# Attention and a max-of-three FFN on one core: another written order of commands, other engines for copies and masks, other places for the K and Q loads

## The chip, the cores and the metric

The kernel runs on one core of a Trainium2 chip. The metric is the device time of one execution in microseconds (us), the median of several runs. A core has five engines that run side by side, each through its own stream of instructions in order, and they wait for one another through semaphores: TensorE (PE in the profile; its weight loads are PEld), VectorE (DVE), ScalarE (ACT), GpSimd (POOL) and SyncE (SP), which here only issues DMAs. DMAs are issued from the queues of SP, POOL and ACT.

## The reference

Two stages. The first is attention of 4 batches with 8 heads over 768 positions and a head size of 64. Heads 0, 2 and 6 ("retrieval") see all earlier positions, the other five only the first 4 positions and the last 64. The second stage takes the 3072 rows of 512 that come out, multiplies them by three matrices, takes the largest of the three products element by element, and multiplies by a fourth matrix.

```python
scores = scale * np.matmul(q, k.transpose(0, 1, 3, 2))
stream_keep = causal & (is_sink | in_win)
scores = np.where(mask[None, :, :, :], scores, -1000000000.0)
a = np.exp(scores - max) / sum
out = np.matmul(a, v)                       # (4, 8, 768, 64)
x = out.transpose(0, 2, 1, 3).reshape(3072, 512)
h = np.maximum(np.maximum(x @ w1, x @ w2), x @ w3)   # (3072, 768)
return h @ w_out                            # (3072, 512)
```

## The kernel before

The work is cut into eight blocks (b,half): batch 0 to 3, first or second half of its 768 positions. Each block has an attention part and an FFN part, and while PE works on the FFN of one block, the attention of the next is woven in between. Nothing is planned at run time: the order is written out by hand in a list of strings, `PROGRAM` (L132). The function `run` (L895) reads it from left to right and emits each command's instructions; each engine gets its own in that order. There is a second list, `GENERAL`, for other patterns of heads; it is in the program behind a branch and isn't run here.

The commands that matter, with the functions behind them. A step t counts batch, half and a bit qd that picks four of the eight heads; i picks two heads of those.

- `ld h hp` loads K and Q of two pairs of heads of batch 0's second half in fp32 (tile kf, `load_pairs`, L293), `load b c` those of four heads of a later batch, cast to fp16 on the way (tile kq, L354). Both go through POOL's queue, in POOL's program order. `w n` loads a weight matrix there too (L556, L563). `load_v b half` loads V in three DMAs from SP, `load_vp` from POOL (tile vs, L412).
- `cast h hp e` casts K and Q of a pair in batch 0 to fp16 (L314), the two letters naming the engines (d DVE, a ACT, p POOL). `turnp h hp e` turns them on PE (L333) and copies them to KQ (L341), with one or two copies. For later batches `turn b qd i part` does the turning with a DVE transposition (L388).
- `s t u` makes scores on PE (tile st, L737) and takes exp on ACT (L748). It uses the two PSUM buffers of the pool sps, or, with a b at its end, buffers of the pool of four banks. `k t i u e` multiplies by the masks on DVE or POOL (L762 for the heads with a window, L782 and L797 for the others). `o` copies the sink columns.
- `v t i e` casts V to fp16 (va, L656) and fills the masked copy vf (L660, L665, L672); the first letter is the engine of the cast, the second that of the copies.
- `av t i` multiplies by V on PE (oacc, L823); DVE then takes the reciprocal of the sums (L831) and writes x (L834).
- `x t i e` transposes x into xT, by PE and a copy (L853, L854), or with D by a DMA from SP (L847). The FFN of a block is put into the queue when its last x is emitted.
- `f 1 e` is one step of the FFN that is first in the queue: four matmuls of 128 by 384 (yy, L591) and then either a copy on engine e (products with the first matrix, L608) or a max on DVE (L611). After 18 such steps come three outputs of six matmuls (L627), each with a copy on engine e (L633) and a DMA from SP (L634), and an empty step behind each. Block (0,·) takes all first products first, the others go round matrix by matrix.
- `gate` and `pad` put a tiny DMA into SP's queue (L398); `gate` waits for a tile of masked scores. `um` makes a mask (L533).

Ahead of the list, K and Q of batch 0's first half are issued from SP and ACT, and constants are made.

What sets who waits for whom: the order on each engine, two score buffers, four PSUM banks for everything else (yy, oacc, transpositions), three buffers of vs and of KQ, four of kf and kq together, two of x and three of xT.

```python
PROGRAM = (
    "um 1 1, cast 0 1 dp, cast 0 3 pd, turnp 0 1 a, cast 0 0 aa, s 0 0 1, ld 1 0, cast 0 2 dd",
    ...
```

Of the kernel before, what the change touches and what calls it, by code (L numbers as in the profile page):

```python
# [129 lines left out]
)  # L130

PROGRAM = (  # L132
    "um 1 1, cast 0 1 dp, cast 0 3 pd, turnp 0 1 a, cast 0 0 aa, s 0 0 1, ld 1 0, cast 0 2 dd",
    "um 0 1, s 0 1 1 b, um 1 0, turnp 0 0 aa, load_v 0 0, turnp 0 3 d, s 0 0 0, turnp 0 2 aa",
    "s 1 0 1, o 0 1 0 d, v 0 0 dd, w 0, v 1 1 dd, ld 1 2, cast 1 0 pp, s 1 1 1, cast 1 1 pp",
    "v 1 0 ad, turnp 1 0 a, w 1, s 0 1 0 b, s 1 0 0, o 0 0 0 p, av 0 0, s 1 1 0 b, av 1 1",
    "av 1 0, v 0 1 pp, um 0 0, turnp 1 1 aa, av 0 1, s 2 0 0, x 0 0 d, s 2 0 1, x 1 0 d",
    "x 0 1 a, load_vp 0 1, x 1 1 d, cast 1 3 aa, cast 1 2 dp, w 2, f 1 a, s 2 1, f 1 a",
    "turnp 1 3 d, load 1 0, f 1 d, f 1 a, s 2 2, f 1 d, turnp 1 2 da, f 1 a, k 2 0 2 d",
    "k 2 0 1 d, k 2 1 1 p, f 1 d, w 3, load 1 1, f 1 a, s 3 0, o 0 0 1 p, o 0 1 1 d, k 3 0 0 d",  # L140
    "f 1 a, v 2 1 dd, v 2 0 ad, v 3 1 ad, f 1 d, v 3 0 dp, s 3 1 0, f 1 d, f 1 d, s 2 3, f 1 a",
    "f 1 d, turn 1 0 0 1, k 3 0 1 p, k 2 0 3 p, f 1 a, f 1 a, k 2 1 3 p, av 2 0, av 3 0, f 1 a",
    "f 1 a, k 3 1 0 p, s 3 1 1, x 3 0 a, x 2 0 a, k 3 1 1 p, turn 1 0 1 0, av 2 1, gate, av 3 1",
    "load 2 0, turn 1 0 0 0, load_v 1 0, f 1 a, x 2 1 a, f 1 a, f 1 a, x 3 1 a, f 1 a, f 1 a",
    "f 1 a, f 1 a, turn 1 1 0 1, turn 1 1 0 0, load 2 1, f 1 a, turn 1 0 1 1, f 1 a",
    "turn 1 1 1 0, turn 1 1 1 1, f 1 d, f 1 a, s 4 0, f 1 d, f 1 a, f 1 d, k 4 0 0 p, s 5 0",
    "f 1 d, k 5 0 0 d, turn 2 0 0 0, k 5 1 0 p, f 1 a, f 1 d, s 5 1, o 1 1 0 p, f 1 a, f 1 a",
    "turn 2 0 1 1, load_v 1 1, s 4 1, f 1 a, o 1 0 0 p, k 4 0 1 d, turn 2 0 1 0, v 5 0 pp",
    "f 1 d, s 5 2, k 4 1 1 p, f 1 a, load_v 3 1, v 5 1 pp, v 4 0 ap, f 1 d, f 1 a, s 6 0",
    "av 4 0, k 4 1 0 d, k 5 1 2 d, v 4 1 dp, f 1 a, k 5 0 2 p, s 6 1, v 7 0 ap, av 5 0",  # L150
    "k 5 0 1 d, av 4 1, x 5 0 D, av 5 1, s 6 2, f 1 a, x 4 1 D, x 4 0 d, f 1 a, turn 2 0 0 1",
    "av 7 0, x 5 1 a, s 6 3, turn 2 1 1 0, k 6 1 1 p, v 6 1 ad, f 1 a, turn 2 1 0 0",
    "turn 2 1 0 1, load 3 1, k 6 0 3 p, f 1 a, f 1 d, k 6 1 3 p, turn 2 1 1 1, f 1 a, k 5 1 1 p",
    "k 6 0 1 p, f 1 d, f 1 a, load_v 2 0, f 1 d, av 6 1, s 8 0, f 1 d, v 7 1 pd, f 1 a, f 1 a",
    "v 6 0 dp, f 1 d, pad, s 9 0, f 1 d, f 1 a, k 8 1 0 d, turn 3 1 1 1, f 1 a, load_v 2 1",
    "f 1 d, k 9 1 0 p, s 8 1, k 6 0 2 p, turn 3 1 1 0, f 1 a, av 7 1, v 8 1 ad, f 1 a, f 1 a",
    "f 1 a, k 9 0 0 d, s 9 1, f 1 d, x 6 1 D, v 9 0 pp, v 9 1 ap, f 1 a, v 10 1 pp, av 6 0",
    "x 6 0 D, turn 3 1 0 0, o 2 1 0 p, s 10 0, x 7 0 D, k 8 0 0 d, o 2 0 0 d, v 11 1 ap, f 1 d",
    "f 1 d, v 14 0 pp, f 1 d, x 7 1 a, f 1 d, turn 3 1 0 1, v 8 0 pd, f 1 d, s 9 2, k 9 1 1 d",
    "pad, v 11 0 dp, k 8 0 1 d, f 1 a, f 1 a, k 9 0 2 d, k 9 1 2 p, f 1 d, f 1 d, f 1 a, f 1 d",  # L160
    "k 8 1 1 d, load_v 3 0, load 3 0, s 10 1, k 10 0 1 p, av 9 0, f 1 a, f 1 a, f 1 d, av 8 1",
    "k 10 1 1 d, s 10 2, v 12 1 pd, av 9 1, x 8 1 D, av 8 0, f 1 a, f 1 d, v 13 0 ap, x 8 0 D",
    "v 10 0 dd, f 1 d, f 1 d, f 1 a, s 10 3, k 9 0 1 d, f 1 d, turn 3 0 0 1, x 9 0 D, f 1 d",
    "x 9 1 D, f 1 a, f 1 a, k 10 0 2 p, f 1 a, turn 3 0 0 0, pad, f 1 d, f 1 d, f 1 a, f 1 a",
    "v 15 0 dp, f 1 a, f 1 d, turn 3 0 1 0, f 1 a, turn 3 0 1 1, f 1 d, av 11 0, v 12 0 ad",
    "k 10 1 3 d, s 12 0, f 1 d, k 10 0 3 p, f 1 a, k 12 0 0 d, f 1 d, f 1 a, s 13 0, v 14 1 pp",
    "av 10 0, f 1 d, f 1 a, s 13 1, av 10 1, k 12 1 0 p, f 1 d, k 13 1 1 p, s 14 0, f 1 d",
    "f 1 d, f 1 d, o 3 0 0 p, f 1 a, f 1 d, v 13 1 ad, s 12 1, k 12 1 1 p, x 11 0 D, x 10 0 D",
    "av 11 1, f 1 a, x 10 1 D, f 1 d, k 12 0 1 d, s 14 1, k 13 0 1 d, f 1 d, f 1 a, k 14 0 1 p",
    "x 11 1 D, f 1 a, o 3 1 0 d, k 13 0 0 d, k 13 1 0 d, f 1 a, f 1 a, av 12 0, f 1 d, s 13 2",  # L170
    "f 1 a, f 1 a, k 13 0 2 p, f 1 a, f 1 a, f 1 d, f 1 a, s 14 2, k 13 1 2 p, av 13 0, f 1 d",
    "x 13 0 D, f 1 a, f 1 d, f 1 d, av 13 1, s 14 3, x 12 0 D, av 12 1, av 15 0, f 1 d",
    "k 14 0 3 d, f 1 a, f 1 a, k 14 1 3 p, f 1 a, f 1 d, f 1 a, k 14 1 1 p, f 1 a, f 1 a",
    "x 12 1 D, v 15 1 pd, k 14 0 2 p, x 13 1 D, f 1 d, f 1 d, f 1 a, av 14 0, x 14 0 D, f 1 d",
    "x 15 0 D, av 14 1, f 1 a, av 15 1, f 1 a, f 1 d, f 1 a, f 1 d, f 1 d, f 1 a, f 1 a, f 1 a",
    "f 1 d, f 1 d, x 14 1 D, f 1 d, f 1 a, f 1 a, f 1 d, f 1 d, f 1 d, f 1 a, f 1 a, f 1 a",
    "x 15 1 D, f 1 d, f 1 d, f 1 a, f 1 a, f 1 d, f 1 d, f 1 a, f 1 a, f 1 d, f 1 a, f 1 d",
    "f 1 d, f 1 d, f 1 d, f 1 d, f 1 d, f 1 d, f 1 a, f 1 d, f 1 a, f 1 d, f 1 a, f 1 a, f 1 d",
    "f 1 d, f 1 a, f 1 a, f 1 a, f 1 a, f 1 d, f 1 a, f 1 a",
)  # L180


# [774 lines left out]
```

## Time and profile before

| what | value |
|---|---|
| median of 6 runs | 195.19 us (192.88 to 196.26) |
| profiled execution | 195.55 us, span of its instructions 193.7 us |
| mean granted clock of PE | 0.992 |
| PE busy | 178.7 us, 92% of the span |
| DVE, ACT, POOL busy | 140.2, 100.7, 80.3 us (72%, 52%, 41%) |
| DMA queues, share of 16 engines | SP 31.4%, POOL 27.4%, ACT 1.7% |
| last instruction of PE ends | 188.07 us |

The profile is of one execution. Its span goes from the first instruction to the last one or the last DMA's end, and 1.85 us of the execution lie outside it. "Busy" is the union of an engine's instructions, "idle before" is the time an engine stood before an instruction, put down to what released it. The chain that ended last is followed back from the end: at each step to what released it. A row in the timeline has start, length, engine, line, operation, result and sources.

### The profile page before, as it was taken

To read this page: it belongs to the slowest core of one execution; us is meant where nothing else is said; L and a number is where in the kernel's file an instruction comes from. 1 tells how busy PE (TensorE), PEld (TensorE's weight loads), DVE (VectorE), ACT (ScalarE), POOL (GpSimd) and SP (SyncE) were. 2 spreads that over 40 slices of the span, in tenths; PEclk is the share of its full clock that TensorE was granted. 3 is DMA by queue.
4 is the path that set the end of the run, shared out by engine and by line. 5 is a ranking of instruction groups with operands and counts; after the bars stand their busy time and mean duration, and the time that the engine had idled before them with its cause. 6 is when DMAs were issued, how large, how long until landed. Compare 5 with 4: busy or idle time off the path is not lost.

```text
span 193.7 us, 4787 instructions
## 1 busy us (share of the span) xinstructions
PE 178.7 (92%) x1887; PEld 104.7 (54%) x1887; DVE 140.2 (72%) x302; ACT 100.7 (52%) x158; POOL 80.3 (41%) x117
## 2 busy tenths in 40 slices
PE   7398799899999888999999999999999999999980
PEld 2265465665555545556565556655565656555540
DVE  4337657999689997699989987677399666638720
ACT  3289898326677991768665448656751111020030
POOL 3289572883268497086495042412807000000000
PEclk9999999999999999999999999999999999999996
DMA  5999999999998359971599940203322151030022
GB/s 157 283 230 239 231 239 213 209 219 214 182 291 186 106 72 258 183 131 33 183 187 166 67 164 3 41 4 95 112 44 42 58 169 24 0 141 22 0 110 65
DMA packets 41277, 26.02 MB, mean 134 GB/s; under 512 B 31586, under 2 KB 36258, under 8 KB 41250
## 3 DMA queue, kind: packets, MB, share of 16 engines
q1 hardware_dynamic: 34994, 14.39, 31.4%
q0 software_dynamic: 4880, 10.23, 27.4%
q10 hardware_dynamic: 1376, 1.05, 1.7%
q8 instruction: 16, 0.26, 0.6%
q14 instruction: 11, 0.09, 0.2%
HBM read 25.17 MB, written 6.29 MB: 162 GB/s over the span
## 4 chain that ended last, share of the span: by engine, by line
PE 71%; DMA 14%; DVE 5%; POOL 4%; issue 2%; ACT 2%; DVEq 0%; SPq 0%; POOLq 0%; ACTq 0%
PE yy L591 40%; PE yy L627 13%; PE st L737 6%; PE oacc L823 6%; DMA kf<-in_q_dram 5%; PE yst L591 3%; DMA ks<-in_k_dram 3%; DMA xT<-x 2%; DMA vs<-in_v_dram 2%; DMA qs<-in_q_dram 1%; POOL kf L293 1%; POOL pn L762 1%; PE yst L627 1%; ACT pn L748 1%; DVE pn L762 1%
## 5 line engine op out<-in xcount | busy, mean ns | idle before, releaser
L591 PE MATMUL yy<-xT,w0t 128*128 128x384 f16 x180 | 36.2, 326 | 2.7 <-DMA xT<-x 1.7
L591 PE MATMUL yy<-xT,w1t 128*128 128x384 f16 x180 | 35.7, 326 | 0.0
L591 PE MATMUL yy<-xT,w2t 128*128 128x384 f16 x180 | 35.5, 326 | 0.0
L748 ACT ACTIVATE pb<-st 128x1024 f16<-128x1024 f32 (+1 forms) x32 | 29.4, 972 | 7.9 <-PE st L737 7.4
L611 DVE TENSOR_TENSOR acc<-yy,acc 128x384 f16<-128x384 f32 x45 | 24.8, 557 | 11.2 <-PE yy L591 6.7
L627 PE MATMUL yy<-woutt,hT 128*128 128x512 f16 (+1 forms) x138 | 31.9, 374 | 0.0
L608 ACT CAST acc<-yy 128x384 f16<-128x384 f32 x29 | 14.0, 483 | 29.1 <-PE yy L591 29.0
L748 ACT ACTIVATE pn<-st 128x1024 f16<-128x1024 f32 (+4 forms) x27 | 22.1, 873 | 11.8 <-PE st L737 11.8
L762 POOL TENSOR_TENSOR pn<-pn,mk 128x512 f16<-128x512 f16 (+3 forms) x14 | 20.8, 1500 | 17.1 <-ACT pn L748 16.9
L611 DVE TENSOR_TENSOR hT<-yy,acc 128x384 f16<-128x384 f32 x45 | 24.6, 556 | 3.3 <-PE yy L591 0.7
L591 PEld LDWEIGHTS <-w0t 128*128 128x128 f16 x192 | 18.1, 98 | 15.7 <-issue 3.8
L388 DVE STREAM_TRANSPOSE KQ<-kq 128x384 f32<-128x384 f32 x24 | 25.4, 1134 | 0.0
L591 PEld LDWEIGHTS <-w1t 128*128 128x128 f16 x192 | 18.0, 98 | 12.2 <-issue 0.3
L591 PEld LDWEIGHTS <-w2t 128*128 128x128 f16 x192 | 18.0, 98 | 11.7 <-issue 0.4
L737 PE MATMUL st<-KQ 32*128 32x128 f16 (+5 forms) x560 | 23.4, 253 | 0.5 <-ACT KQ L341 0.5
L627 PEld LDWEIGHTS <-hT 128*128 128x128 f16 x150 | 14.0, 98 | 14.2 <-issue 0.3
L633 ACT COPY ot<-yy 128x512 f32<-128x512 f32 x16 | 9.4, 590 | 18.3 <-PE yy L627 18.3
L834 DVE TENSOR_TENSOR x<-oacc,rc 128x384 f16<-128x384 f32 x32 | 17.8, 558 | 1.5 <-DVE rc L831 0.4
L737 PEld LDWEIGHTS <-KQ 32*128 32x128 f16 (+1 forms) x560 | 11.6, 93 | 13.1 <-issue 8.8
L748 ACT ACTIVATE pa<-st 128x1024 f16<-128x1024 f32 (+2 forms) x18 | 12.4, 745 | 6.1 <-PE st L737 5.1
L665 POOL COPY vf<-va 64x390 f16<-64x390 f16 (+1 forms) x10 | 5.2, 519 | 15.4 <-DVE va L656 11.6
L608 DVE CAST acc<-yy 128x384 f16<-128x384 f32 x16 | 8.9, 555 | 3.7 <-PE yy L591 3.5
(96 smaller groups left out, 207.6 us busy)
## 6 DMA issues: line engine op xcount, KB each, us to landing
out_dram<-ot SPq DMA_DIRECT2D x23, 256.0 KB, 2.2
vs<-in_v_dram SPq DMA_DIRECT2D x21, 256.0 KB, 5.1
kq<-in_k_dram POOLq DMA_DIRECT2D x3, 384.0 KB, 7.0
kq<-in_q_dram POOLq DMA_DIRECT2D x3, 384.0 KB, 9.8
kq<-in_k_dram POOLq DMA_DIRECT2D x3, 288.0 KB, 9.3
kq<-in_q_dram POOLq DMA_DIRECT2D x3, 288.0 KB, 11.4
qs<-in_q_dram ACTq DMA_DIRECT2D x4, 192.0 KB, 5.2
ks<-in_k_dram SPq DMA_DIRECT2D x4, 192.0 KB, 5.4
```

The lines of the kernel that those rows point to most:

```text
L388: nc.vector.transpose(out=dst.rearrange("c (p j) -> c j p", j=n)[:, j0:j1], in_=src.rearrange("c (j i) -> c j i", i=R),)
L591: nc.tensor.matmul(yy[:, 0:HALF], w_t[wi][:, ks, ni * P : (ni + 1) * P], xT[b, half][ks].rearrange("p a t -> p (a t)"), start=(ks == 0), s ...
L608: copy_out[0](out=acc[ni], in_=yy[:, 0:HALF])
L611: nc.vector.tensor_tensor(out=dst, in0=yy[:, 0:HALF], in1=acc[ni], op=ALU.max)
L627: nc.tensor.matmul(yo[:, 0:n], hT[ns][:, tb * P : (tb + 1) * P], woutt[:, ns, c : c + n], start=(ns == 0), stop=(ns == NNB - 1),)
L633: op(out=ot[:, c : c + n], in_=yo[:, 0:n])
L665: copy(out=vf[j][D:P, hs, k0 - 1 : k1 - 1, 0 : D + 1], in_=va[j][D:P, hs, k0:k1, 0 : D + 1],)
L737: nc.tensor.matmul(sts[g // m][:, g % m, c0 : c0 + n * P], KQ[r0 : r0 + nr, 0, abs(ki) * P : (abs(ki) + 1) * P], KQ[r0 : r0 + nr, 1, q0 * ...
L748: nc.scalar.activation(out=pts[of_step(t, i)][:, h0 : h0 + m, off : off + w], in_=st[:, :, 0:w], func=AF.Exp, scale=sc,)
L762: engine.tensor_tensor(out=x, in0=x, in1=m.to_broadcast([P, 2, r, n]), op=ALU.mult)
L823: nc.tensor.matmul(o[:, qi, hl, 0 : D + 1], pt[:, hl, c : c + P], vv[:, 0 : D + 1], start=(idx == 0), stop=(idx == len(todo) - 1), skip_gr ...
L834: nc.vector.tensor_tensor(out=xs[b, half][:, i : i + 3 : 2, :, qd].rearrange("p h a d -> p a h d"), in0=o[:, :, :, 0:D], in1=rc.unsqueeze( ...
```

## The change

The 47 strings of `PROGRAM` are replaced by 47 others. Nothing else in the file changes. The commands are the same but for three things: `pad` occurs once instead of three times, and two more x are transposed by DMA (23 instead of 21); engines are dealt out anew. Letters of copies and masks: mask commands on DVE 24 before and 36 after, on POOL 30 and 18; FFN steps marked a 106 and 102, d 86 and 90 (the mark counts only in steps that copy). POOL's loads stand in the order `ld 1 0`, `w 0`, `ld 1 2`, `w 1`, `load_vp 0 1`, `w 2`, `load 1 0`, `w 3`, `load 1 1` before, and `ld 1 0`, `ld 1 2`, `w 0`, `load_vp 0 1`, `w 1`, `w 2`, `w 3`, `load 1 0`, `load 1 1` after. The start, and the stretch around the first two FFN blocks:

```diff
-    "um 1 1, cast 0 1 dp, cast 0 3 pd, turnp 0 1 a, cast 0 0 aa, s 0 0 1, ld 1 0, cast 0 2 dd",
-    "um 0 1, s 0 1 1 b, um 1 0, turnp 0 0 aa, load_v 0 0, turnp 0 3 d, s 0 0 0, turnp 0 2 aa",
-    "s 1 0 1, o 0 1 0 d, v 0 0 dd, w 0, v 1 1 dd, ld 1 2, cast 1 0 pp, s 1 1 1, cast 1 1 pp",
-    "v 1 0 ad, turnp 1 0 a, w 1, s 0 1 0 b, s 1 0 0, o 0 0 0 p, av 0 0, s 1 1 0 b, av 1 1",
-    "av 1 0, v 0 1 pp, um 0 0, turnp 1 1 aa, av 0 1, s 2 0 0, x 0 0 d, s 2 0 1, x 1 0 d",
-    "x 0 1 a, load_vp 0 1, x 1 1 d, cast 1 3 aa, cast 1 2 dp, w 2, f 1 a, s 2 1, f 1 a",
...
-    "load 2 0, turn 1 0 0 0, load_v 1 0, f 1 a, x 2 1 a, f 1 a, f 1 a, x 3 1 a, f 1 a, f 1 a",
-    "f 1 a, f 1 a, turn 1 1 0 1, turn 1 1 0 0, load 2 1, f 1 a, turn 1 0 1 1, f 1 a",
-    "turn 1 1 1 0, turn 1 1 1 1, f 1 d, f 1 a, s 4 0, f 1 d, f 1 a, f 1 d, k 4 0 0 p, s 5 0",
...
+    "cast 0 0 ad, load_v 0 0, cast 0 1 pp, ld 1 0, um 1 1, turnp 0 1 aa, um 1 0, cast 0 3 pa",
+    "um 0 1, s 0 0 1, s 0 1 1 b, turnp 0 3 a, cast 0 2 pp, ld 1 2, turnp 0 0 ad, turnp 0 2 ad",
+    "um 0 0, cast 1 1 dd, s 0 0 0, cast 1 0 dd, w 0, s 1 0 0, s 0 1 0 b, load_vp 0 1, o 0 0 0 p",
+    "v 0 1 dd, v 1 1 dd, v 0 0 dp, turnp 1 0 d, turnp 1 1 da, s 1 0 1, av 0 0, w 1, av 0 1",
+    "o 0 1 0 p, cast 1 2 pa, s 1 1 1, s 1 1 0 b, s 2 0 1, v 1 0 pp, cast 1 3 ap, av 1 1",
+    "s 2 0 0, av 1 0, x 1 0 d, x 0 0 a, turnp 1 2 dd, s 2 1, x 0 1 d, w 2, x 1 1 d, turnp 1 3 d",
+    "f 1 d, s 3 0, k 2 0 1 d, f 1 d, k 3 0 0 d, w 3, o 0 0 1 p, s 3 1 0, k 3 1 0 d, f 1 a",
...
+    "av 2 0, f 1 a, f 1 d, load 1 1, x 2 0 a, x 3 0 a, f 1 a, load_v 1 0, load 2 0",
+    "turn 1 0 0 0, f 1 d, turn 1 0 0 1, x 2 1 a, turn 1 0 1 0, x 3 1 a, f 1 a, f 1 d, f 1 a",
+    "turn 1 0 1 1, turn 1 1 0 1, f 1 a, f 1 a, f 1 a, f 1 a, f 1 a, turn 1 1 0 0, f 1 a",
+    "turn 1 1 1 1, f 1 a, turn 1 1 1 0, f 1 d, turn 2 0 0 0, load_v 1 1, s 5 0, k 5 0 0 p",
+    "f 1 a, load 2 1, f 1 d, f 1 d, s 4 0, turn 2 0 1 1, f 1 a, k 4 0 0 d, f 1 d, f 1 d, s 5 1",
+    "o 1 0 0 d, f 1 d, f 1 a, k 4 1 0 d, s 4 1, k 5 1 0 d, o 1 1 0 p, v 5 0 pp, f 1 a, s 5 2",
+    "v 4 0 dp, k 4 0 1 d, f 1 a, k 4 1 1 d, k 5 0 2 d, f 1 d, av 4 0, v 4 1 pd, v 5 1 ap",
+    "turn 2 0 0 1, s 6 0, f 1 a, k 5 1 2 p, av 5 0, v 6 0 dd, av 4 1, s 6 1, x 4 0 D, f 1 a",
...
```

## The prediction

> **What bounds the kernel now.** First the page: busy times, then the 40 slices (4.84 us each).
>
> ```profile
> PE 178.7 (92%) x1887; PEld 104.7 (54%) x1887; DVE 140.2 (72%) x302; ACT 100.7 (52%) x158; POOL 80.3 (41%) x117
> ...
> PE   7398799899999888999999999999999999999980
> DVE  4337657999689997699989987677399666638720
> ...
> DMA  5999999999998359971599940203322151030022
> ```
>
> TensorE (PE) is busy in 9 tenths or more of nearly every slice after the fourth; DVE is next, with its dense slices between the ninth and the twentieth. The DMA engines are full from the second slice to the twelfth. So PE sets the time, and what can be won lies where PE waits. To see where, I cut the span at marks that both orders pass: the first FFN product of block (0,0) (23.10), its first output product (42.44), the first product of block (1,0) (73.40, counted without the wait inside it), the first of block (1,1) (94.96), the last PE instruction (188.07).
>
> ```profile
> 23.10:42.44 19.34, 18.46 (x212) 11.39 (x212) 14.47 (x32) 12.56 (x21) 13.12 (x19) 1.00 1.13 219
> 42.44:73.40 30.96, 28.85 (x343) 15.97 (x340) 27.66 (x50) 23.20 (x34) 19.18 (x32) 1.00 0.85 179
> 73.40:94.96 21.56, 21.40 (x279) 12.78 (x279) 18.30 (x39) 12.25 (x19) 11.43 (x17) 1.00 0.67 151
> 94.96:188.07 93.11, 93.10 (x901) 55.04 (x900) 66.84 (x139) 38.20 (x57) 23.36 (x25) 1.00 0.34 77
> 188.07:193.70 5.63, 0.00 (x0) 0.00 (x0) 0.42 (x1) 0.00 (x0) 0.00 (x0) 0.73 0.29 101
> ```
>
> The third number of a row is PE's busy time, the next pairs are weight loads, DVE, ACT, POOL. Against this I set the PE work of each stretch, from the command list and the rows: an FFN step is 4 matmuls in 0.65 us, an output 6 matmuls in 1.29, a score step of later batches 0.36 to 0.57, an `av` 0.032 per matmul, a transposition of x 0.17, of K or Q 0.17 each. That gives 17.5, 26.6, 21.1 and 92.4 us of work; the stretches took 19.3, 31.0, 21.6 and 93.1. So 1.8, 4.4, 0.5 and 0.7 us were lost, and the first 23.1 us are start-up. The second half runs at PE's own pace; nothing can be won there, only lost. The waits of PE name part of the loss (last number: longest):
>
> ```profile
> PE yy L591 <- DMA xT<-x: 1.7, 1, 1.7
> PE yy L591 <- ACT xT L854: 1.0, 1, 1.0
> PE oacc L823 <- DVE va L656: 0.6, 1, 0.6
> ```
>
> The chain of waits shows the two places where PE is not the chain (start, length, what):
>
> ```profile
> 12.43 10.11 DMA kf<-in_q_dram
> ...
> 63.88 1.39 DVE pa L782 x2
> 65.27 0.60 DVE pn L762
> ...
> 68.70 0.03 DVE xT L854
> 68.73 4.79 DMA xT<-x
> ```
>
> At the start the chain is the K and Q loads; at 63.6 to 73.5 it is DVE, which finishes the attention of block (1,0) late, so the x that becomes xT leaves late, and its DMA takes 4.79 us.
>
> **The change, part by part.** Counting both lists: the instructions are the same but for engines and order. Of the 68 mask instructions 15 go from POOL to DVE (35 and 33 become 20 and 48). Two more xT go by DMA (21 become 23), so PE does 2 x 0.17 = 0.3 us less. Two small `pad` DMAs go. FFN copies barely move (ACT 47 to 49). K and Q loads stay on POOL's queue; only their place in it changes.
>
> *Start-up.* The loads `ld 1 0` are now behind the two casts of pair (0,1), not behind that of pair (0,3): in the trace ks of pair 1 was cast from 6.82 and that of pair 3 from 8.80, so POOL issues at 7.8 instead of 9.25. `ld 1 2` comes before `w 0`. The DMA share is 1.07 from 8 to 23 us, so an earlier issue brings little: before, the first Q cast started on its landing at 14.69; I take 13.9 (bounds 13.3 and 14.7). kf of pairs 2 and 3 landed at 22.5 behind w0 (19.25), 3.3 later; now ahead of it, at 17.2. w0 took 4.65 after the load ahead of it, so it lands at 21.9; `load_vp 0 1` now stands before `w 1`, 3.3 more; w1 took 3.7 (22.5 to 26.2), so 28.9. It is needed at the seventh step, near 30: it just fits, and if it doesn't, PE waits for all that is late.
> From 13.9 the chain is now DVE, in its order: four casts at 0.47 from start to start (8.94, 9.41 in the trace), 1.9; the v copies 1.5; KQ copies 0.9 + 0.5; four `av` ends (0.23 + 0.47 each) 2.8; one xT 0.3; the two KQ halves of pair 2, 0.95; two xT 0.6. Sum 9.4, so the first FFN step starts at 23.3, against 23.1 before. If the listed durations (0.55 for a cast, 0.56 for an x) follow each other whole, some 20 instructions cost 0.08 more each: 24.9. If loads come at 13.3: 22.7. But PE has then done more: turnp 1 2, turnp 1 3 and a score step lie ahead of the mark, so 7.1 us of work instead of 5.9, and the rest is 16.3 + 26.1 + 21.4 + 92.4 = 156.2 instead of 157.6.
>
> *First block.* Work 16.3. Score steps 3 0, 2 2 and 2 3 each need both score banks, freed by two exps of 0.95; ACT gets its K and Q casts earlier but still has some 11 us of exps there. I add 1.2 for that and 1.0 for the switches between kinds of matmul that cost before too: 18.5, against 19.3. The output starts at 41.8.
>
> *Blocks (0,0) out to (1,0).* All eight KQ transposes (six took 5.89 from 43.34, 0.98 each) now stand before the first max of block (0,1), while its copies go to ACT: 8 us of DVE under 9 us of PE, so hidden; without that cover PE would wait for a bank after four tiles. kq (1,1) must land by 45.5; what is queued ahead of it (w2, w3, kq (1,0)) had landed by 40.4 before, and a pair takes some 4 us: 44.5. `load_v 1 0` moves on SP from behind the gate (40.6) to behind the first output, near 43, and v of block (1,0) is wanted at 58: hidden. DVE has 31.0 us by listed durations in this stretch, as before (31.1), because the masks gained are offset by v copies that go to POOL. One named wait is new: `k 5 1 2 p`, 2.12 on POOL behind v 5 1, in front of `av 5 1`: 0.5. What was paid for late va (0.6) goes, since `load_v 1 1` is queued earlier. The three xT DMAs of block (1,0) start behind output (0,1) on SP; at 1.2 us issue and 2.4 us landing (median of the 21) they are there 0.3 late. With one more wait of 0.7 for exps before s 6 3 I book 3.0 lost of 26.1 (bounds 1.5 and 5.5, the upper with DMAs at 4.79): 29.1 against 31.0. Block (1,0) starts at 70.9.
>
> *The rest.* 21.4 + 0.5 to block (1,1), at 92.8; 92.4 + 0.7 to the end: 185.9 for PE, against 188.07. All `av` there have their last mask two or more steps ahead. The tail is untouched, 5.63 us: span 191.5.
>
> *Masks that meet.* A DVE mask that starts inside a POOL mask is held up:
>
> ```profile
> 62.80 2.12 POOL L762 TENSOR_TENSOR pn<-pn,mk 128x1024 f16<-128x1024 f16 x1
> ...
> 63.88 1.39 DVE L782 TENSOR_TENSOR pa<-pa,base 128x256 f16<-128x256 f16 x2
> ```
>
> Two masks of 256 took 1.39 us, 0.48 at 82.21 us; three more were stretched, by 0.6, 0.2 and 0.9. That is 2.6 us over 33 DVE masks with 41 us of POOL masks. After: 48 with 23.5 us, 2.6 x 48/33 x 23.5/41 = 2.2. No term for it. The Trainium skill ("SBUF — State Buffer", Who interferes with whom) speaks against such a move: a DVE instruction with two SBUF inputs and a POOL instruction that reads SBUF exclude each other for a whole instruction. The trace agrees, 63.88 ending only after POOL's at 64.92. By the rule at its worst, each of 15 more masks meeting half a POOL mask, an estimate would be 9 us more on DVE, which has 53 us idle; by the rows it is nothing.
>
> *Sum.* 185.9 - 188.07 = -2.2 us. The profiled run took 195.55, span 193.7; so 193.4. The median is 195.19, 0.36 lower: 193.0. A measurement here can tell about 1% (2 us) from nothing.
>
> **The rivals.** *Nothing gained* (0.28): the DMA engines are full until 42 us either way and the K and Q loads stay on one queue, so moving them does not do what it says, and DVE's start-up chain runs at listed durations: 24.9 (+1.6), and 0.5 more in the second stretch: PE ends at 188.0, time 195.1. For it: DVE has 3 us more work before the first step than before. Against: the same trace shows starts 0.47 apart. *Slower, xT by DMA* (0.24): every block from (1,0) on takes xT by DMA through SP, in order, three or four at 1.2 us after the last `av`. Slack by the lists: none in (1,0), 1.7 us in (1,1), 1.1 in (3,0). At the 4.79 of 68.73 instead of 2.4 us they cost 2.4 + 0.7 + 1.3 = 4.4: 197.4; at 5.7, which four had in this trace, 3.3 + 1.6 + 2.2 = 7.1: 200.1. It eats the gain from a landing of 4.0 us on. Against: the slow ones ran beside K, Q or v loads, and the new list has none due at these three places but `load 3 0`.
>
> **How the numbers follow.** The forecast, 0.48. Its own bounds are 22.7 and 24.9 at the start and 1.5 and 5.5 in the second stretch: 190.9 to 197.1. The range reaches to 189.5, if the first block loses 0.8 instead of 2.2 too, and to 198.0, which takes in the slower case at its first price. Faster by over 1% 0.48, within 1% 0.28, slower 0.24.
>
> **What would show it.** Right: first FFN product near 23.3, first output near 41.8, block (1,0) near 71, (1,1) near 93, then 93 us to the last PE instruction; no wait for xT over 0.5; DVE masks 48. Wrong: a first product after 25; waits of yy for xT of 2 us or more; PE idle behind w1 near 29 or behind a KQ transpose; any loss after (1,1).

## The result and the profile after

The new list takes 193.96 us (median of 33 runs, 192.68 to 195.72), the old one in the same runs 195.24 (70 runs). The ratio is 0.9956, with a 95% interval from 0.9939 to 0.9974: about 0.9 us faster, less than the 1% that the forecast counted as a difference. The ratio leaves out runs in a slower state, over 1.5% above the fastest of their own list, and is not the quotient of the two medians, which is 0.9934 (1.3 us). The forecast was 193.0 us, 0.989 of the old time. The profiled execution of the new list took 195.02 us, 1.06 above its own median, with a span of 193.2.

The page of the new list (busy times, then the 40 slices of 4.83 us):

```profile
PE 180.3 (93%) x1881; PEld 105.7 (55%) x1881; DVE 145.4 (75%) x312; ACT 98.6 (51%) x150; POOL 66.8 (35%) x114
...
PE   7687899999999999999969999999999999999990
...
DVE  4138899999899989978998898858789577616720
...
PEclk9996999999999999999999999999999999999999
```

The holes of PE in the eighth slice and in the fourteenth to the sixteenth are gone. Two things are new: a 6 in PE's twenty-first slice (96.6 to 101.4 us), and a 6 in the granted clock in the fourth. The stretches between the forecast's marks, here the first FFN product (24.77), the first output product (42.34), the first products of blocks (1,0) and (1,1) (71.12, 93.02) and the end of PE (188.59):

```profile
0.00:24.77 24.77, 19.01 (x180) 11.47 (x181) 13.28 (x47) 15.16 (x27) 15.84 (x33) 0.93 1.02 244
24.77:42.34 17.57, 17.33 (x195) 10.70 (x193) 16.36 (x40) 8.66 (x13) 7.20 (x13) 1.00 1.14 207
42.34:71.12 28.78, 28.43 (x324) 15.49 (x322) 26.81 (x48) 22.45 (x34) 13.73 (x21) 1.00 0.68 151
71.12:93.02 21.90, 21.90 (x290) 13.06 (x289) 19.24 (x36) 15.47 (x23) 9.47 (x18) 1.00 0.87 165
93.02:188.59 95.57, 93.66 (x901) 54.98 (x899) 69.31 (x144) 36.89 (x56) 20.52 (x30) 1.00 0.35 84
188.59:193.20 4.61, 0.00 (x0) 0.00 (x0) 0.42 (x1) 0.00 (x0) 0.00 (x0) 1.00 0.34 121
```

The second and third numbers of a row are its length and PE's busy time. From the first output to (1,1) PE now stands still for 0.35 us in 50.68; in the old list it was 2.3 in 52.5. But the last row but one, which lost nothing before (93.10 busy of 93.11), now loses 1.9. The waits of PE after 93 us name what it stood for:

```profile
PE yy L591 <- DVE x L834: 1.2, 1, 1.2
PE yy L591 <- DVE acc L611: 0.4, 1, 0.4
PE yy L591 <- DMA xT<-x: 0.3, 1, 0.3
```

The first two lie at 97 to 100 us, and DVE is late there. Its instructions and POOL's in that place:

```profile
93.37 0.23 POOL L672 COPY vf<-va 4x65 f16<-4x65 f16 x1 [7.66 <-ACT va L656]
93.57 1.78 POOL L797 TENSOR_TENSOR pa<-pa,mk 128x512 f16<-128x512 f16 x2
...
93.40 2.23 DVE L762 TENSOR_TENSOR pn<-pn,mk 128x512 f16<-128x512 f16 x1
...
97.94 0.55 POOL L656 CAST va<-vs 128x384 f16<-128x384 f32 x1 [2.59 <-DMA vs<-in_v_dram]
...
98.04 1.37 DVE L762 TENSOR_TENSOR pn<-pn,mk 128x512 f16<-128x512 f16 x2
99.33 0.18 DVE L831 RECIPROCAL rc<-oacc 128x6 f32<-128x6 f32 x1
99.55 0.56 DVE L834 TENSOR_TENSOR x<-oacc,rc 128x384 f16<-128x384 f32 x1
```

A DVE mask of 128 x 512, which takes 0.42 us alone, started at 93.40 and took 2.23: it ended 0.28 after POOL's copy and two masks. At 98.04 two more, 0.75 together when undisturbed, took 1.37 beside POOL's casts. DVE was busy for 8.57 of the 8.80 us from 92.4 to 101.2, the held time included, so little absorbed this; x came at 100.1, and the next FFN product, which needs the PSUM bank that DVE had to empty, waited 1.20 us. The first row also shows why POOL did its mask just then: it had stood for 7.66 us in front of a copy that waited for a cast of ACT, with the mask queued behind, whose scores had been ready since 79.4.

### The profile page after: what moved, and what is told of

The parts are those of the page before. It is cut to its first block, busy times and chain, and to the rows that moved or that the text cites. A ratio compares the mean times of both kernels' runs of the same rounds, so it can differ in the third digit from the quotient of the medians.

```text
span 193.2 us, 4762 instructions
## 1 busy us (share of the span) xinstructions
PE 180.3 (93%) x1881; PEld 105.7 (55%) x1881; DVE 145.4 (75%) x312; ACT 98.6 (51%) x150; POOL 66.8 (35%) x114
## 4 chain that ended last, share of the span: by engine, by line
PE 78%; DMA 11%; DVE 4%; ACT 2%; issue 1%; POOL 1%; SPq 0%; ACTq 0%; DVEq 0%
PE yy L591 44%; PE yy L627 13%; PE st L737 9%; PE oacc L823 8%; DMA kf<-in_q_dram 3%; PE yst L591 3%; DMA out_dram<-ot 3%; DMA xT<-x 2%; DMA ks<-in_k_dram 2%; ACT pb L748 1%; DVE KQ L341 1%; DVE x L834 1%; PE yst L627 1%; PE tr L853 1%; DVE pn L762 1%
## 5 line engine op out<-in xcount | busy, mean ns | idle before, releaser
L608 ACT CAST acc<-yy 128x384 f16<-128x384 f32 x28 | 13.5, 482 | 31.7 <-PE yy L591 26.4
L611 DVE TENSOR_TENSOR hT<-yy,acc 128x384 f16<-128x384 f32 x45 | 24.9, 556 | 3.6 <-PE yy L591 0.8
L737 PE MATMUL st<-KQ 32*128 32x128 f16 (+5 forms) x560 | 24.4, 254 | 0.7 <-ACT pa L748 0.2
L737 PEld LDWEIGHTS <-KQ 32*128 32x128 f16 (+1 forms) x560 | 12.0, 93 | 13.7 <-issue 10.8
L633 ACT COPY ot<-yy 128x512 f32<-128x512 f32 x17 | 10.0, 589 | 17.3 <-PE yy L627 13.9
L762 POOL TENSOR_TENSOR pn<-pn,mk 128x512 f16<-128x512 f16 (+2 forms) x7 | 11.0, 1569 | 22.2 <-ACT pn L748 14.6
L762 DVE TENSOR_TENSOR pn<-pn,mk 128x512 f16<-128x512 f16 (+3 forms) x23 | 13.5, 620 | 1.0 <-ACT pn L748 1.0
L656 POOL CAST va<-vs 128x384 f16<-128x384 f32 x14 | 7.8, 562 | 12.3 <-DMA vs<-in_v_dram 12.0
```

What stands on the lines that cost most here:

```text
L608: copy_out[0](out=acc[ni], in_=yy[:, 0:HALF])
L611: nc.vector.tensor_tensor(out=dst, in0=yy[:, 0:HALF], in1=acc[ni], op=ALU.max)
L633: op(out=ot[:, c : c + n], in_=yo[:, 0:n])
L656: op(out=va[j][:, hs, k0 : k0 + HB, 0:D], in_=vs[:, hs])
L737: nc.tensor.matmul(sts[g // m][:, g % m, c0 : c0 + n * P], KQ[r0 : r0 + nr, 0, abs(ki) * P : (abs(ki) + 1) * P], KQ[r0 : r0 + nr, 1, q0 * ...
L762: engine.tensor_tensor(out=x, in0=x, in1=m.to_broadcast([P, 2, r, n]), op=ALU.mult)
```

## The experiments

Theory A: the loss after 93 us is the meeting of POOL's and DVE's masks. Its rivals: B, DVE has too many masks there, whoever else runs; and chance of one execution. The second question was where the 1.6 us before 93 come from, the third what the start and the tail do. In all these runs the commands are also spread over the strings in another way. That moves one thing only, a branch hint that `run` puts ahead of the last four strings: 36 commands are left behind it, 45 and 43 in the old and the new list. e0 and e6, each the same commands as one of the two lists, bear out that the stretches between the marks don't hang on it.

**e0: the new list again.**

> The new list once more, nothing edited. Theory A (the 2.0 us that PE stands or crawls between 96 and 100.2 us belong to the order): a second profile has the same marks within 0.3 us (first FFN product 24.8, first output 42.5, block (1,0) 71.1, block (1,1) 93.0, last PE instruction 188.6), a DVE mask of 512 of over 2 us near 93.4 and a PE wait of about 1.2 us for x near 100. Rival B (chance of one execution): the marks up to 93 move by over 0.5 us or the wait near 100 is gone. The tail of 4.54 us against 5.63 in the old list is expected to be scatter of the last DMAs: between 4.4 and 5.8. Time 0.9956 of before, within 0.003.

Measured: 193.86 us, 0.9928 of before (0.9895 to 0.9961). The length of the stretches came back to 0.03 us (17.54, 28.78, 21.91) and the rest to 0.26 (95.31); the held mask took 2.23 us again, and PE's waits were 1.5 and 0.4. So it is not chance. The start did not come back: first FFN product at 25.34, first output at 42.88. The tail (from the end of PE to the end of the span) was 4.62, against 4.61.

**e3: POOL's masks of step 8 earlier.**

```diff
-    ... v 8 0 ap, f 1 d, f 1 a, k 8 0 0 p, k 9 0 0 d, ...
+    ... k 8 0 0 p, v 8 0 ap, f 1 d, f 1 a, k 9 0 0 d, ...
```

> The new list with one command moved: the masks of step 8 (first pair, POOL, 1.8 us) stand ahead of the V cast of step 8 instead of behind it, so that POOL does them near 86 us, where it stood waiting for ACT's cast, and not at 93.57 under DVE's masks of step 9. Theory A (the two masks exclude each other): the DVE mask that took 2.23 us takes 0.42 to 0.7, PE's waits of 1.20 and 0.35 us near 97 to 100 shrink to under 0.6 together, (1,1) to the last PE instruction takes 94.1 to 94.6 instead of 95.6, time 0.9935 or less of the new list's 1 (0.988 to 0.990 of before). Rival B (DVE has too many masks there, whoever else runs): the waits stay at 1.3 us or more and the time is that of the new list within 0.002.

Measured: 192.64 us, 0.9865 (0.9832 to 0.9897), measured side by side with e0. The last stretch took 93.15 us, as in the old list; no wait of PE is left after (1,1). Even the second meeting, at 98, went with the first, since DVE was no longer late. But POOL's two masks now ran at 84.56, and met something else:

```profile
84.56 1.77 POOL L797 TENSOR_TENSOR pa<-pa,mk 128x512 f16<-128x512 f16 x2
...
85.29 1.25 DVE L378 COPY KQ<-KQ 32x32 f16<-32x32 f16 x2
...
PE yy L627 <- DVE hT L611: 0.7, 1, 0.7
```

Two small copies, 0.35 us in the new list, took 1.25; DVE's max behind them came late, PE waited 0.7 for its hT at 88.15, and (1,0) to (1,1) took 22.77 instead of 21.90.

**e4: the same masks on DVE.** This is the test between A and B, since DVE gets more work.

```diff
-    ... k 8 0 0 p, ...
+    ... k 8 0 0 d, ...
```

> The new list with one letter changed: the masks of step 8, first pair, go from POOL to DVE as well, at their place in the list. That is 0.7 us more work for DVE in the very stretch where it was late, and no POOL mask is left that the four DVE masks of step 9 could meet. Theory A (meeting): DVE saves the 1.8 us of the held mask and pays 0.7, the KQ sink copies of 0.35 stay as they are, PE's waits near 97 to 100 go from 1.55 us to 0.5 or less, (1,1) to the last PE instruction takes 93.1 to 93.9, time 0.985 to 0.990 of before, like the run with the masks moved early. Rival B (load): DVE falls back 0.7 further, the waits grow to 2.2 us and the time is 0.996 or more.

Measured: 192.49 us, 0.9898 (0.9864 to 0.9932). The place of the held mask, and the last stretch:

```profile
92.37 0.68 DVE L797 TENSOR_TENSOR pa<-pa,mk 128x512 f16<-128x512 f16 x2
92.98 0.75 DVE L762 TENSOR_TENSOR pn<-pn,mk 128x512 f16<-128x512 f16 x2
...
92.32:185.61 93.29, 93.29 (x901) 54.91 (x899) 67.27 (x146) 36.89 (x56) 18.48 (x28) 1.00 0.35 85
```

The four masks take 1.4 us together, and PE is busy for all of 93.29. DVE has more instructions (146 for 144) and less busy time (67.27 for 69.31). B has fallen: giving DVE more work freed it. From the first FFN product to (1,1) its stretches are those of the new list to 0.01 us, so this is the new list without its one loss.

**e1: new start, old rest.** In this and the next two the list is cut at an FFN step: the commands of one list up to there, then all that are left, in the other's order and with its engines. The seam:

```diff
     ... x 1 1 d, turnp 1 3 d,        (new list)
-    f 1 d, s 3 0, k 2 0 1 d, f 1 d, k 3 0 0 d, ...
+    f 1 a, f 1 a, load 1 0, f 1 d, f 1 a, s 2 2, ...        (what is left, old order)
```

> The new list up to the first FFN step, then all commands that are left in the old list's order and with its engines. If the start as such is what came late: first FFN product at 24.8 (old 23.1). What is then left of the first block is the new list's 16.3 us of work plus the old losses, so the first output comes at 42.5 to 43.3, block (1,0) at 73.5 to 74.3 as in the old list, and the time is 0.998 to 1.004 of before: the new start brings nothing by itself. Rival: the early loads (pairs 2 and 3 ahead of the first matrix) are worth something in the old rest too: first output at 41.5 or earlier, time 0.995 or less.

Measured: 194.81 us, 1.0005 (0.9976 to 1.0033). The start brings nothing by itself that these runs can tell. Its trace has the first FFN product at 23.39, though, not at 24.8, and the first output at 41.58. What differs is the granted clock. First the new list, then e1 (the granted clock is the third number from the end of a row):

```profile
14.00:16.00 2.00, 0.58 (x6) 0.21 (x5) 1.45 (x4) 1.41 (x3) 1.02 (x2) 1.00 1.05 287
16.00:17.00 1.00, 0.92 (x10) 0.92 (x11) 0.95 (x5) 0.00 (x0) 0.00 (x0) 0.60 1.13 206
17.00:18.00 1.00, 1.00 (x8) 0.47 (x7) 0.99 (x3) 0.48 (x1) 0.46 (x2) 0.50 1.16 210
18.00:19.00 1.00, 1.00 (x17) 0.74 (x17) 0.80 (x2) 0.41 (x1) 0.91 (x3) 0.50 1.16 216
```

```profile
17.00:18.00 1.00, 0.99 (x30) 0.86 (x26) 1.00 (x3) 0.86 (x1) 0.89 (x2) 1.00 1.16 212
18.00:19.00 1.00, 0.78 (x13) 0.38 (x10) 0.96 (x4) 0.93 (x4) 1.00 (x4) 1.00 1.16 213
```

In the new list's profile PE's clock fell to half from 16.2 to 19.6, just where scores and products with V stand in front of DVE: the 24 matmuls of the first two `av` took 1.33 us there, against 0.75 for the same number later in the same trace.

**e2 and e8: both cuts at the first FFN step of (1,0).** e2 is new before and old after, e8 old before and new after (with the letter of e4).

```diff
     ... s 6 3, turn 2 1 1 1, turn 2 1 1 0,        (e2: new list)
-    f 1 a, v 6 1 pd, f 1 a, k 6 1 3 p, ...
+    load_v 3 1, av 7 0, v 6 1 ad, turn 2 1 0 0, ...        (what is left, old order)
```

> The new list up to the first FFN step of block (1,0), then the old order and engines for what is left. Theory (the gain lies before 71 us and is given back after 93): block (1,0) starts at 71.1, (1,1) 21.6 later at 92.7, PE ends 93.1 later at 185.8, span 190.4 to 191.4 with a tail of 4.5 to 5.6, time 0.985 to 0.990 of before. Rival (the gain before 71 was borrowed, DVE or the loads come late afterwards whatever the rest is): PE ends at 187.5 or later, with new waits of PE between 71 and 110, time 0.994 or more.

> The reverse cut: the old list up to the first FFN step of block (1,0), then what is left in the new order and with its engines, with the masks of step 8, first pair, on DVE. From the first output to the first product of (1,1) the old list takes 52.2 to 52.5 us, the new one 50.7; new up to (1,0) and old from there took 52.4. Theory P (the gain of 1.6 us is made by the new order of block (1,0) and what it prepares): 50.7 to 51.3 here, time 0.988 to 0.993 of before. Rival Q (it takes the new order on both sides of the cut, since what one side leaves late the other has to do): 52 or more, time 0.996 to 1.000.

Measured: e2 193.73 us, 0.9939 (0.9902 to 0.9976); e8 195.59 us, 1.0025 (0.9991 to 1.0060). From the first output to (1,1), in e8 and in e2:

```profile
43.32:95.85 52.53, 50.37 (x618) 28.68 (x615) 44.13 (x81) 37.00 (x54) 27.08 (x44) 1.00 0.83 168
```

```profile
40.87:93.26 52.39, 50.69 (x615) 28.86 (x613) 47.71 (x89) 36.95 (x56) 27.19 (x42) 1.00 0.78 170
```

Both take as long as the old list, so theory P fell and the 1.6 us did not survive a cut here, whichever half was new, as Q said. PE's waits say why. e8 has the old ones, 1.4 for xT by DMA and 0.6 for va. e2 has neither, but 1.3 for masks and V copies on POOL (0.6, 0.4, 0.3) that the old order asks for right after the cut. The seam has a share in that: in e2 `load_v 3 1`, `av 7 0` and `v 6 1` stand together right behind the cut, as in neither list, and no run tells the seam from the old order. e2's own gain is the first block (17.57 us, with the new start e1 took 18.19) and a PE end at 186.4 without the meeting.

**e5: the old list with xT of two x by PE.**

```diff
-    ... x 5 0 D, av 5 1, s 6 2, f 1 a, x 4 1 D, ...
+    ... x 5 0 d, av 5 1, s 6 2, f 1 a, x 4 1 a, ...
```

> The old list with two letters changed: x of steps 4 (second pair) and 5 (first pair) become xT by PE and a copy (ACT, DVE), not by DMA, so that no DMA stands between the attention of block (1,0) and its FFN. If the wait of 1.65 us for that DMA is what the new list gains around 71 us: 1.65 less the two transpositions of 0.17 and some 0.3 for the copies, so (1,1) starts at 93.9 instead of 94.96 and the time is 0.993 to 0.996 of before. Rival: DVE's lateness behind it (the held mask of 1.39 us and the KQ transpositions) takes the place of the wait: time within 0.002 of before.

Measured: 194.98 us, 0.9988 (0.9944 to 1.0032): the rival. The wait for the DMA was gone, and the output part in front of it took 30.61 instead of 29.14 us, since PE now waited 0.9 us for x in order to transpose it. First output to (1,1): 52.11 for 52.2 and 52.5. So the old list's 1.65 us at xT are not the DMA's alone: DVE has the block's last x 26.3 us after the first output (25.6 in the new list, 26.5 here), and PE waits for it in whichever way it is transposed.

**e6: the old list again.**

> The old list once more, nothing edited, for the scatter of the marks: first FFN product 22.5 to 24.5, block (1,0) 73 to 74.5 counted without a wait for xT, last PE instruction 93.1 after (1,1), tail between 4.4 and 5.8. If the granted clock falls to half for some us in the first 26 us here too, such falls belong to the start of either list; if it stays at 1.00, they may belong to the new one.

Measured: 194.94 us, 1.0017 (0.9974 to 1.0060). First output to (1,1) 52.20, rest 93.17, tail 6.18, PE's first FFN product at 21.24 with 1.0 us of waiting behind its first matmul; the clock stayed at 1.00. It fell in other runs of the old start (e5, 0.50 from 7.7 to 14.5 us), so falls are no property of the new one.

**e7: the start reordered on PE,** on top of e4.

```diff
-    ... turnp 1 1 da, s 1 0 1, av 0 0, w 1, av 0 1, ... s 1 1 0 b, s 2 0 1, v 1 0 pp, cast 1 3 ap, av 1 1, ...
+    ... turnp 1 1 da, av 0 0, w 1, av 0 1, s 1 0 1, ... s 1 1 0 b, v 1 0 pp, cast 1 3 ap, av 1 1, s 2 0 1, ...
```

> The run with the masks of step 8 on DVE, and two score commands of the start moved: that of step 1 (pair 0) from ahead of the first product with V of step 0 to behind the second one, that of step 2 from ahead of the products of step 1 to behind them. Theory (at a full clock DVE waits 0.2 to 0.9 us for PE in its chain from the landing of K and Q to the first x, because scores stand ahead of the products): first FFN product 22.9 to 23.3 where the unmoved start has 23.3 to 23.7, time 0.002 less than without the move. Rival (the exps that come later hold the products of step 1 instead): first FFN product at 23.7 or later, time the same or more.

Measured: 193.73 us, 0.9952 (0.9913 to 0.9991), first FFN product at 24.92 at a clock of 1.00: the rival. The first x came no earlier (4.4 us after the cast of the Q that landed, as in e1), since DVE's copies of KQ stand ahead of it, and then DVE waited 1.13 us for the `av` of step 1, whose scores and exps now come later.

**e9: old start, new rest (with e4's letter),** and **e10: the old list with the new one's letters in the last FFN block.**

```diff
     ... x 1 1 d, cast 1 3 aa, cast 1 2 dp, w 2,        (e9: old list)
-    f 1 a, s 2 1, f 1 a, turnp 1 3 d, ...
+    turnp 1 2 dd, s 2 1, turnp 1 3 d, f 1 d, s 3 0, ...        (what is left, new order)
```

```diff
-    f: d a d d d d d d d a d a d a a d d a a a a d a a        (e10: the last 24)
+    f: d d d a a d a a a d a d a a d a a a a d a d d d
```

> The old list up to the first FFN step, then the rest in the new order, with the masks of step 8, first pair, on DVE. If the start itself is worth nothing (as the new start with the old rest said, 1.0005 of before): first output at 41.8 to 42.5 as in the old list, then 50.7 to (1,1), 93.2 to the last PE instruction at 185.7 to 186.4, tail 4.7, time 0.987 to 0.992, the same as with the new start. If the new start is worth something only together with the new rest (pairs 2 and 3 loaded early): first output 43 or later, time 0.994 or more.

> The old list with the engine letters of the last FFN block's steps as in the new list (16 letters differ). The tail (end of PE to end of span) was 5.1 to 6.2 us in the five traces of lists that end in the old order, 4.6 to 4.8 in the five that end in the new one. If the copies of the last block make it: tail 4.6 to 4.8, time 0.994 to 0.997 of before. If not (where loads of instructions fall, or what stands earlier in the queues): tail 5.1 to 6.2, time within 0.002 of before.

Measured: e9 192.72 us in four runs, 0.9845 (0.9796 to 0.9894), with stretches of 50.69 and 93.30: the new rest does as well behind the old start. e10 195.15 us, 0.9993 (0.9965 to 1.0022), tail 5.95: the last copies don't make the tail.

What the marks were, from the traces ("rest" is from (1,1) to the end of PE, "tail" from there to the end of the span):

| list | first output | to (1,1) | rest | tail | time to before |
|---|---|---|---|---|---|
| old (two traces) | 42.44, 41.95 | 52.5, 52.2 | 93.2, 93.2 | 5.6, 6.2 | 1 |
| new (two traces) | 42.34, 42.88 | 50.7, 50.7 | 95.6, 95.3 | 4.6, 4.6 | 0.9956 |
| e3, mask early | 41.22 | 51.6 | 93.2 | 4.7 | 0.9865 |
| e4, mask to DVE | 41.64 | 50.7 | 93.3 | 4.7 | 0.9898 |
| e9, old start | 42.34 | 50.7 | 93.3 | 4.7 | 0.9845 |
| e1, old rest | 41.58 | 52.3 | 93.2 | 5.1 | 1.0005 |

e3, e4 and e9 beat both lists, by 1.0 to 1.6% of the old one. Their intervals overlap, so which of them is best is not settled; that of e4 also reaches into that of e0 (0.9895 to 0.9961), so for e4 the gain over the new list rests on the stretch of 93.3 us as well.

## Why the prediction was right or wrong

**The step that failed** is "Masks that meet", with its "No term for it". It scaled the held time of the old trace to 2.2 us and called the price nothing, with DVE's 53 us of idle time in the whole span as the room. The amount was too low, though that alone did not decide: summed over what each takes above its undisturbed duration (0.28, 0.42, 0.55 and 0.69 us for 256, 512, 768 and 1024), DVE's masks were held for 3.7 us in the new list and 2.9 in the old. The mistake was to look for room in the span's sum. Of the 3.7, 2.4 fell on a stretch of 8.8 us in which DVE, with the held time, had 0.2 to spare, and nearly all of it came out at PE: 95.4 us in the mean of the two traces instead of 93.2 (e3 and e4 give that back; 0.3 of it, in one trace, is a wait for xT). The old list has a hold of 0.9 in its last stretch too:

```profile
145.97 1.31 DVE L797 TENSOR_TENSOR pb<-pb,mk 128x512 f16<-128x512 f16 x1
```

It cost PE nothing, for PE was busy for 93.10 of the 93.11 us of that stretch, although DVE was busy for 6.58 of the 7.00 us from 143 to 150. So a little room was enough there: what counts is the size of the hold, the room, and how soon PE needs what DVE does next.

By the forecast's own words it is wrong with "any loss after (1,1)", and that came; "All `av` there have their last mask two or more steps ahead" was counted in the list, without the time that POOL would stand in front of one.

The rule that the prediction weighed and left out of the sum pointed the right way: the Trainium skill ("SBUF — State Buffer", Who interferes with whom) says that such a DVE and such a POOL instruction exclude each other for a whole instruction. The traces agree, and go further: at 93.40 one DVE mask was held through three POOL instructions that followed without a gap, 1.8 us. The 9 us that the prediction estimated from it at the worst were far above the 3.7 that came.

**The start** (forecast: 23.3, K and Q of pairs 0 and 1 at 13.9, DVE's chain 9.4 behind it) was right in the chain where the clock stood at 1.00 behind the landing: in e1, e2, e3 and e4, which share this start, the cast behind the landing began at 14.12, 14.04, 14.39 and 14.81, and the first FFN product came 9.3 later, at 23.39, 23.30, 23.66 and 24.07. In the two profiles of the new list the cast began at 14.55 and 14.57 and the chain took 10.2 and 10.8, with the clock at half for 3.4 us of it or more. No run sets the clock, so that it made the difference is likely, not shown. That DVE's chain would run at full durations (the first rival's 24.9) is not what e1 to e4 show. The earlier loads were worth less than forecast: that cast began at 14.40 in the mean of the seven traces with the new loads and at 14.63 in that of the six with the old ones, so 0.2 us earlier, not 0.8.

Two marks of the prediction were misread. At 23.10 the old list has its second FFN matmul; the first ran at 21.73, and PE then waited 1.04 us for an xT, where the new list goes on without a wait. And block (1,1) begins at 94.90 there, not at 94.96, which makes its last stretch 93.17 us.

**The first block** was booked with 2.2 us of losses and lost 1.3: 17.57 us, not 18.5, within 0.03 in all lists with the new start and block. PE is busy for 17.33 of it, so the 1.0 booked for switches is there and the 1.2 booked for the exps is not. Of start and block together, 0.64 us earlier than before were forecast. The first output comes at 41.8 in the mean of the five traces with the new start and block (40.87 to 42.88), at 42.3 in that of the five with the old ones (41.80 to 43.32): some 0.5 earlier, under the scatter of the start.

**First output to (1,1)** was right: 51.0 forecast (41.8 to 92.8), 50.68 measured, within 0.02 in the traces of the new list, e0, e4 and e9. The waits that the forecast named for the old list (xT, va) are gone. Its parts are not as booked, though. Of the named waits (0.5 behind POOL's mask, 0.3 for xT, 0.7 for exps) only 0.2 for an exp is left. Up to block (1,0) PE is instead busy for 28.43 us with what the forecast counted as 26.1 of work; the old list has 28.85 for 26.6. So the sum of single durations falls short by 2.3 us in both, and that the booked 3.0 fitted is in part luck. e5 bears out that DVE's late x stands behind the old list's wait for xT, more than the DMA.

**The tail** was "untouched". It is 4.4 to 4.8 us in the seven traces whose second half is in the new order and 5.1 to 6.2 in the six whose second half is in the old one. e10 rules out the last copies. The DMA packets of the traces show where it lies: the packets of the last output end 3.5 to 4.0 us after PE in the four traces with a tail of 5.6 or more (old, e5, e6, e10) and 2.1 to 2.7 us after it in the other nine; from there 2.2 to 2.8 us are left to the end. In these four alone a load of 16 KB of instructions starts 1.4 to 1.7 us after PE's end, beside that output; in e1 and e8 it starts at 2.0 or later, and in the other seven none falls there. No run moved that load, so the cause stays open. The tail is worth about 1 us, and by the sum below the new list would hardly have been faster without it.

So the sum, in means over the traces: -2.2 became -0.5 for start and block, -1.6 to (1,1), +2.3 in the rest and -1.1 in the tail, -0.9 in all. The e4 list, without the failed step, is where the forecast had put the new one: 192.49 for 193.0, with the last PE instruction at 185.6 for 185.9. Luck has a part in that: its first FFN product is 0.8 late, its first block 0.9 short, and its tail 0.9 shorter than assumed.

**The rivals.** "Nothing gained" gave the right size, and was right that the early loads bring little (0.2 us); but DVE's start-up chain ran as forecast in e1 to e4, and the loss lay after (1,1), where this rival had none. "xT by DMA late" did not come: the landings took 2.3 us in the median, the longest 4.6, and PE waited for xT once, 0.34 us at 155.67. (The longest of the old list is 6.7, where the prediction says 5.7.)

## What to carry to other kernels

Room on an engine is a property of a stretch, not of the span: before a cost is set at nothing, look for the place where it will fall, and ask what the engine's idle time is between there and the next thing that PE waits for. When masks go to DVE while POOL keeps some, look at what stands in front of POOL's: an instruction that waits for another engine can hold POOL's later work back until it meets DVE's. And an order that wins in one stretch may need the stretches around it, so test cuts on both sides before saying where a gain was made, and remember that the seam of a cut is an order of its own.

## What was not expected of the hardware

A DVE mask was held for as long as POOL had work without a gap (2.23 us for 0.42, in two executions), not for one POOL instruction. Two DVE masks were held beside casts on POOL too (1.37 for 0.75), and two DVE copies of 32 x 32 beside a POOL mask (1.25 for 0.35).

The granted clock falls to 0.50 for some us in the first 26 us of some executions, of both lists, and not of others with the same instructions: in the new list from 16.2 to 19.6, in e0 from 8.1 to 15.0 and from 21.8 to 25.2, in e2 from 7.4 to 10.9, in e4 from 8.4 to 11.8, in e5, e9 and e10 (old start) from about 8 to 15, in e8 (old start) from 8.9 to 19.1, never in e1, e3, e6 or e7. Each fall lasts 3.4 us or two or three times that. The falls that ended before 12 us, in e2 and e4, left the chain of the start at 9.3 us; with those between 16 and 26 us it took 0.95 and 1.5 us more, about as much as this change was worth. The Trainium skill ("TensorE: Matmul & The Clock Gate", What's actually happening) describes a gate that halves the clock after an idle window of about 3.4 us which runs freely; the halving, the lengths and the chance in it agree with the traces. The idle window does not: PE was busy for 1.92 of the 3.42 us before the fall at 16.2, and for 2.33 of the 3.41 us before the one at 21.8 in e0.
